# Making VectorE's lower halves of the expert weights one group later, in a one-core attention, routing and expert kernel

## The chip, the cores and the metric

The kernel runs on one core of a Trainium2 chip. A core has a matrix engine (TensorE, PE in the profile), VectorE (DVE), ScalarE (ACT), GpSimd (POOL) and a sync engine (SP) that mostly starts DMAs. Each engine works through its own instruction list in order; semaphores make one wait for another. The metric is the device time of one execution in microseconds (us), lower is better.

## What is computed

The reference, cut to the part that the change touches:

```python
# x: 2304 tokens of 512, from an attention stage; logits = x @ w_gate, 8 experts of 288 tokens each,
# tokens and experts matched greedily by descending logit
for e in range(8):
    h = np.maximum(x[mask_e] @ w1[e], 0.0)     # 512 -> 1024
    out[mask_e] = h @ w2[e]                    # 1024 -> 512
h = out @ w_in                                 # 512 -> 2048
g = np.maximum(h, 0.0) + np.log1p(np.exp(-np.abs(h)))   # softplus
return g @ w_out                               # 2048 -> 512
```

## The kernel before

Attention runs first (to about 205 us), then one pass over the experts e = 0 to 7, each with its 288 tokens. Every fp32 matrix is split in two fp32r tiles: an **upper half**, written by a ScalarE copy that rounds, and a **lower half**, which VectorE makes as the difference of the original and the upper half. A product is three matmuls into one PSUM bank (`mm3`, lines 913 to 915): upper by upper, upper by lower, lower by upper. In an expert product L913 and L914 need only the upper half of the weights, and L915 needs the lower half too.

Expert e has two loops:

- The **first loop** has 8 iterations. Iteration i makes hidden block i + 2 (`H1`: 12 matmuls into a bank of a ring of three, then a ScalarE Relu as upper half and a VectorE instruction, L1103, as lower half) and adds block i to the result (`Y`, 12 matmuls). Before `H1` it splits block i + 3 of `w1`, and after it block i + 4 of `w2` (i + 2 for expert 1).
- The **second loop** has 16 iterations. Iteration i makes block i + 2 of the second product (`H2`, 12 matmuls into the same ring), puts block i through softplus and adds it to the output (`O`). Softplus is three ScalarE functions, then `upper()`: VectorE L1148 and a ScalarE copy L1149, and `lower()`: VectorE L1157, which is also the last reader of the bank. In iterations 10 to 13 the next expert's tokens are transposed through a ring bank (`xpose`, L1075, and its VectorE half L1081), and in 9 to 15 the first blocks of the next expert's `w1` and `w2` are split. Iterations 14 and 15 hold the next expert's `H1` of blocks 0 and 1.

`split_w` (ScalarE L1026, VectorE L1029) reads a raw block that `load_w` brought from HBM. There are two raw buffers for `w1` and two for `w2`, so the load of block n + 2 can start when the lower half of block n is made. These loads are issued by SP. GpSimd issues the loads of the output weights `wo` (512 KB each), which start when `O` frees a buffer.

Between these, `tick` interleaves the **router**, which finds the next expert's tokens while this one computes. A router step of the **long kind** is a PE matmul L707 and a VectorE chain from L709 to L682; one of the **short kind** is five small PE matmuls L690 and a VectorE chain L694, L700, L702. L690 needs the result of L682, and L707 that of L702. Each half of an iteration has one `tick`, some of them empty. The router has finished for all experts at about 715 us.

`then` appends a VectorE instruction to a list when the list is in use, and `now` works the list off. Before the change it holds the lower halves of `H1` and of the transposes.

Of the kernel before, what the change touches and what calls it, by code (L numbers as in the profile page):

```python
# [8 lines left out]
F32 = mybir.dt.float32  # L9
# [5 lines left out]
ALU = mybir.AluOpType  # L15
# [544 lines left out]
class Router:  # L560


    def __init__(r, g, pool, work, bank, ring):
        r.g, r.pool, r.work, r.ring = g, pool, work, ring
        nc = g.nc
        r.n = 0
        r.idxk = g.rcf[:, 0:18]
        r.steps = [g.rcf[:, 18 + 32 * i : 50 + 32 * i] for i in range(5)]
        r.rank = g.rcf[:, 178:186]
        r.eix = g.rcf[:, 186:194]  # L570
        r.iota = g.rcf[:, 194:322]
        r.last32 = g.rcf[:, 322:323]
        r.ones16 = g.rch[:, 0:128]
        r.own4 = g.rch[:, 128:132]
        r.fine = False
        r.tri = g.rcb[:, 0:128]
        r.ones = g.rcb[:, 128:256]
        r.warm = g.rcb[:, 0:256]
        r.uw = g.rcb[:, 256:292].rearrange("p (c k) -> p c k", k=2)

        r.bank, r.used = bank, 0
        r.L = pool.tile([P, NCOL, E], F32, name="rL")
        big = r.place(31 * E + 32)
        r.oh0 = big[:, 0 : NCOL * E].rearrange("p (c e) -> p c e", e=E)
        r.m = big[:, 144:162]
        r.col = big[:, 162 : 162 + E]
        r.cnt = big[:, 0 : 31 * E]
        r.part = big[:, 31 * E :]
        r.own31 = r.place(31)
        r.key, r.loi, r.hi, r.lo, r.inc, r.free, r.pos, r.blk, r.pp = (r.place(NCOL) for _ in range(9))  # L590
        r.full, r.kp, r.pc, r.pn = r.place(E), r.place(E), r.place(E), r.place(1)
        r.pi = r.place(6)
        nc.vector.tensor_copy(r.own31, g.rch[:, 132:163])
        r.x = pool.tile([P, 5, E], F16, name="rx")
        nc.gpsimd.memset(r.x, 0.0)
        r.now = g.L
        r.k = pool.tile([P, E], F32, name="rk")
        r.kneg = pool.tile([P, 2, E], BF, name="rkneg")
        nc.gpsimd.memset(r.kneg[:, 0], -float(CAP))
        nc.gpsimd.memset(r.kneg[:, 1], 0.0)  # L600
        nc.gpsimd.memset(r.k, float(CAP))
        r.row = pool.tile([P, P], BF, name="rrow")
        nc.gpsimd.memset(r.row, 0.0)
        nc.gpsimd.memset(r.row[0:1, :], 1.0)
        r.cmp = pool.tile([P, 2, 9 * 32 + 96], BF, name="rcmp")
        nc.gpsimd.memset(r.cmp[:, :, 9 * 32 :], 0.0)
        r.all = pool.tile([P, 5 * P], BF, name="rall")
        nc.gpsimd.memset(r.all[:, NCOL * 32 :], 0.0)
        r.pw = pool.tile([P, 5, P], BF, name="rpw")
        nc.gpsimd.memset(r.pw, 0.0)  # L610
        for i in range(5):
            nc.gpsimd.memset(r.pw[0:31, i, :], float(32**i))
        r.asg = pool.tile([P, NCOL, E], BF, name="rasg")
        nc.gpsimd.memset(r.asg, 0.0)
# [259 lines left out]
class FFN:  # L874
# [141 lines left out]
            )  # L1016
        (f.w1 if which == 1 else f.w2)[e, fb] = raw

    def split_w(f, e, which, fb):
        nc = f.nc  # L1020
        d = f.w1 if which == 1 else f.w2
        raw = d[e, fb]

        tag = "w1" if which == 1 else "wo" if e and (8 * e + fb) % 5 < 3 else "w2"
        h = f.t([P, 2, 512], F32R, tag, 2 if tag == "w2" else 3)
        nc.scalar.activation(h[:, 0], raw, AF.Copy)  # L1026

        if e:
            nc.vector.tensor_tensor(h[:, 1], raw, h[:, 0].bitcast(F32), op=ALU.subtract)  # L1029
        else:  # L1030
            for c in (slice(0, 256), slice(256, 512)):
                nc.gpsimd.tensor_tensor(h[:, 1, c], raw[:, c], h[:, 0, c].bitcast(F32), op=ALU.subtract)
        d[e, fb] = h[:, 0], h[:, 1]

    def split_out(f, e, fb):

# [181 lines left out]
    def run(f):  # L1218
        nc = f.nc
# [37 lines left out]
        def tails(i):  # L1257

            if i == TL - 2:
                for _ in range(3):  # L1260
                    f.load_tail()
            if i >= TL:
                if f.ntail == 4 * NG - 4:
                    need(24)
                    f.wl = f.last()
                if f.ntail < 4 * NG:
                    f.late += 0.6 if f.ntail >= TP else 0.0
                    f.split_tail()
# [36 lines left out]
        f.tails, f.ntail = [], 0  # L1305
        for e in range(STOP):
            more = e + 1 < E
            if e:
                f.late_ops = []
            for i in range(8):  # L1310
                if i + 3 < 8:
                    f.split_w(e, 1, i + 3)
                if i + 5 < 8:
                    f.load_w(e, 1, i + 5)
                if i + 2 < 8:
                    f.H1(e, i + 2)
                tick(0.4, i < 7, e > 1)
                f.now()
                a = 4 if e > 1 else 2
                if e and i + a < 8:  # L1320
                    f.split_w(e, 2, i + a)
                if e == 0:
                    tails(i - 8)
                f.Y(e, i)
                if i % 2:
                    f.load_out(16 * e + 4 + i // 2)
                if not e and i + a < 8:
                    f.split_w(e, 2, i + a)
                if i + a + 2 < 8:
                    f.load_w(e, 2, i + a + 2)  # L1330
                if i < 7:
                    tick(0.0, True, e > 1)
            f.evac_y()
# [12 lines left out]
            for i in range(16):  # L1346
# [4 lines left out]
                elif more:  # L1351
                    f.H1(e + 1, i - 14)
                tick(0.0, i < 15, False, e == 0)
                f.now()
                if e == 0 and i + 2 < 16:
                    f.split_out(e, i + 2)
                    f.G()
                if e and i + 1 < 16:
                    f.lower()
                if e == 0:  # L1360
                    tails(i)
                    need(2 * i + 9 + LD)
# [12 lines left out]
                if more:  # L1375
                    if i == (U1 if e else U0):
                        until(e + 1)
                        f.gather(e + 1)
                        f.first_w(e + 1)
                    a, b = (10, 11) if e else (11, 14)  # L1380
                    if e and i >= 9:
                        w = (1, 0), (2, 0), (1, 1), (2, 1), (1, 2), (2, 2), (2, 3)
                        f.split_w(e + 1, *w[i - 9])
                        f.load_w(e + 1, w[i - 9][0], w[i - 9][1] + 2)
                    if not e and a <= i < a + 3:
                        f.split_w(e + 1, 1, i - a)
                        f.load_w(e + 1, 1, i - a + 2)
                    if not e and b <= i:
                        f.split_w(e + 1, 2, i - b)
                        f.load_w(e + 1, 2, i - b + 2)  # L1390
                if e == 0 and 8 <= i < 12:
                    f.load_out(i + 8)
            f.evac_o(e)
# [50 lines left out]
```

## Time and profile before

| | |
|---|---|
| median of 3 runs | 918.45 us (915.64 to 919.82) |
| profiled execution | 918.4 us, of which 916.4 us are its span |
| mean granted TensorE clock | 0.963 of 2.4 GHz |
| PE busy | 837.3 us, 91% of the span, 7152 matmuls |
| DVE busy | 595.3 us, 65% |
| ACT busy | 470.6 us, 51% |
| POOL busy | 292.4 us, 32% |

The profiled execution lies 0.05 us from the median and is taken as its picture. First loops begin about where ScalarE and VectorE copy out the output of the expert before (for experts 1 to 7 at 313.1, 403.0, 488.1, 581.1, 666.4, 751.6 and 827.4 us) and end with the split of their result (at 340.3, 426.6, 511.4, 605.2, 694.4, 773.0 and 849.1 us); the second loops lie between. A matmul's row ends by a model, later than the next one's usual start, so lateness on PE is read from start to start: 0.13 us from one matmul of 288 columns to the next, 0.23 us of 512.

### The profile page before, as it was taken

The page shows a single profiled execution, that of the slowest core. Times are in us where ns is not written, and L with a number is a line of the kernel's source. Part 1 is how long each engine was busy: PE and PEld are TensorE (multiplying, and loading weights), DVE is VectorE, ACT ScalarE, POOL GpSimd, SP SyncE. Part 2 cuts the span into 40 slices and gives each one's busy share as a digit, 9 for nine tenths or more (in the row PEclk, how much of TensorE's full clock was granted, in tenths as well). Part 3 has the DMA queues.
Part 4 walks back from the last instruction along what each step waited for, and adds up shares of the span by engine and source line. Part 5 has one row for each costly group of instructions (what it writes and reads, how often), then busy time and mean ns, then how long its engine had stood idle before and what let it go on. Part 6 is the DMA issues. An engine that isn't in the chain of part 4 may idle for free.

```text
span 916.4 us, 19578 instructions
## 1 busy us (share of the span) xinstructions
PE 837.3 (91%) x7152; PEld 740.0 (81%) x7152; DVE 595.3 (65%) x1700; ACT 470.6 (51%) x1187; POOL 292.4 (32%) x483
## 2 busy tenths in 40 slices
PE   8796989748898999989999999999889999999996
PEld 6675778637886888879878987898789899989985
DVE  4586968698867787666767565767766763344322
ACT  4675767315575535544554444445534564663542
POOL 7567431218866303310321131114101420321211
PEclk9998989859999999999999999999999999999998
DMA  9988888835256926750766165618552864665330
GB/s 256 263 264 271 247 241 269 275 113 147 93 207 244 288 70 183 208 184 27 226 179 197 46 203 157 196 28 263 149 174 56 248 202 142 184 187 185 98 109 35
DMA packets 91039, 163.03 MB, mean 178 GB/s; under 512 B 9448, under 2 KB 46824, under 8 KB 90560
## 3 DMA queue, kind: packets, MB, share of 16 engines
q1 hardware_dynamic: 66688, 85.71, 30.0%
q0 software_dynamic: 19104, 68.17, 25.0%
q10 hardware_dynamic: 5152, 7.92, 3.1%
q8 instruction: 56, 0.92, 0.4%
q14 instruction: 39, 0.32, 0.1%
HBM read 140.66 MB, written 21.10 MB: 177 GB/s over the span
## 4 chain that ended last, share of the span: by engine, by line
PE 63%; DMA 13%; DVE 13%; issue 5%; ACT 4%; POOL 2%; SPq 0%; ACTq 0%; DVEq 0%; POOLq 0%
PE ring L913 9%; PE ring L915 9%; PE acc L913 9%; PE ring L914 9%; PE acc L914 8%; PE acc L915 8%; DMA raw<-in_w_dram 5%; DMA vraw<-in_vr_dram 2%; DMA craw<-in_wout_dram 2%; PE SD L314 1%; DVE w L1029 1%; PE OD L341 1%; DMA xr<-xs,ridx 1%; PE TD L332 1%; ACT w L1026 1%
## 5 line engine op out<-in xcount | busy, mean ns | idle before, releaser
L1159 POOL CAST rem<-hh 128x64 fp32r<-128x64 f32 x128 | 32.5, 254 | 419.0 <-DVE hh L1157 407.7
L1149 ACT ACTIVATE hh<-ring 128x288 fp32r<-128x288 f32 x128 | 52.7, 412 | 134.3 <-DVE ring L1148 125.7
L913 PE MATMUL ring<-yth,wih 128*128 128x288 f32 x384 | 115.5, 301 | 0.0
L914 PE MATMUL ring<-ytl,wih 128*128 128x288 f32 x384 | 113.7, 296 | 0.8 <-DVE ytl L1123 0.8
L915 PE MATMUL ring<-yth,wil 128*128 128x288 f32 x384 | 112.9, 294 | 0.0
L913 PE MATMUL acc<-wo,hh 128*128 128x512 f32 x256 | 106.3, 415 | 0.0
L1148 DVE SCALAR_TENSOR_TENSOR ring<-ring,t 128x288 f32<-128x288 f32 x128 | 59.0, 461 | 72.7 <-ACT t L1137 72.0
L915 PE MATMUL acc<-wo,hh 128*128 128x512 f32 x256 | 100.8, 394 | 0.7 <-DVE hh L1157 0.7
L914 PE MATMUL acc<-wo,hh 128*128 128x512 f32 x256 | 100.6, 393 | 0.0
L913 PE MATMUL ring<-xgh,w 128*128 128x288 f32 x256 | 78.5, 307 | 4.1 <-DVE hh L1157 2.3
L915 PE MATMUL ring<-xgh,w 128*128 128x288 f32 x256 | 76.9, 300 | 4.0 <-DVE w L1029 3.1
L1157 DVE TENSOR_TENSOR hh<-ring,hh 128x288 fp32r<-128x288 f32 x128 | 58.0, 454 | 31.3 <-ACT hh L1149 30.4
L1051 POOL DMA_DIRECT2D wo<-wh x112 | 60.6, 543 | 55.6 <-PE acc L915 37.1
L1135 ACT ACTIVATE t<-ring 128x288 f32<-128x288 f32 x128 | 52.3, 409 | 49.2 <-PE ring L915 47.6
L1029 DVE TENSOR_TENSOR w<-raw,w 128x512 fp32r<-128x512 f32 x79 | 54.1, 689 | 35.6 <-ACT w L1026 35.1
L914 PE MATMUL ring<-xgl,w 128*128 128x288 f32 x256 | 76.1, 297 | 1.2 <-DVE xgl L1081 1.2
L913 PEld LDWEIGHTS ring<-yth,wih 128*128 128x128 f32 x384 | 72.2, 188 | 3.2 <-issue 1.3
L914 PEld LDWEIGHTS ring<-ytl,wih 128*128 128x128 f32 x384 | 72.2, 188 | 3.0 <-DVE ytl L1123 1.3
L1026 ACT ACTIVATE w<-raw 128x512 fp32r<-128x512 f32 x95 | 58.6, 626 | 29.6 <-DMA raw<-in_w_dram 25.6
L915 PEld LDWEIGHTS ring<-yth,wil 128*128 128x128 f32 x384 | 72.4, 188 | 0.0
L1101 ACT ACTIVATE hh<-ring 128x288 fp32r<-128x288 f32 x64 | 26.2, 409 | 80.6 <-PE ring L915 80.1
L1136 ACT ACTIVATE t<-t 128x288 f32<-128x288 f32 x128 | 57.0, 445 | 4.0
(245 smaller groups left out, 2295.6 us busy)
## 6 DMA issues: line engine op xcount, KB each, us to landing
wo<-wh POOLq DMA_DIRECT2D x112, 512.0 KB, 4.2
raw<-in_w_dram SPq DMA_DIRECT2D x128, 256.0 KB
craw<-in_wout_dram SPq DMA_DIRECT2D x16, 512.0 KB
wh<-wo SPq DMA_DIRECT2D x16, 512.0 KB
vz<-in_vw_dram ACTq DMA_DIRECT2D x36, 142.2 KB
vraw<-in_vr_dram SPq DMA_DIRECT2D x16, 288.0 KB
dnx<-dn SPq DMA_DIRECT2D x36, 128.0 KB
qg<-in_qc_dram SPq DMA_DIRECT2D x11, 384.0 KB
```

The costliest lines, as they stand in the source:

```text
L913: nc.tensor.matmul(o, a[0], b[0], start=start, stop=False)
L914: nc.tensor.matmul(o, a[0], b[1], start=False, stop=False)
L915: nc.tensor.matmul(o, a[1], b[0], start=False, stop=stop)
L1026: nc.scalar.activation(h[:, 0], raw, AF.Copy)
L1029: nc.vector.tensor_tensor(h[:, 1], raw, h[:, 0].bitcast(F32), op=ALU.subtract)
L1051: f.nc.gpsimd.dma_start(out=h, in_=f.g.wh[:, fb])
L1135: nc.scalar.activation(t1, o, AF.Abs)
L1136: nc.scalar.activation(t2, t1, AF.Exp, scale=-1.0)
L1148: nc.vector.scalar_tensor_tensor(o, o, 0.0, t1, op0=ALU.max, op1=ALU.add)
L1149: nc.scalar.activation(h[:, 0], o, AF.Copy)
L1157: nc.vector.tensor_tensor(h[:, 1], o, h[:, 0].bitcast(F32), op=ALU.subtract)
L1159: nc.gpsimd.tensor_copy(f.rem[fb][:, :, c : c + 32], h[:, :, 2 * P : CAP])
```

## The change

- `split_w` still issues ScalarE's upper half at once, but the VectorE lower half, with the load that follows it, goes into the list of `then` (for expert 0 there is no list and nothing changes). The list runs at the next `now`: half an iteration to an iteration later, behind the router step of the `tick` that stands ahead of that `now`.
- In the second loop `lower()` is called ahead of `now` and no longer behind it.
- The list is made once, ahead of expert 1, and not anew for each expert, so that an entry of the last iteration is carried over.
- One copy of 31 columns at the router's start (`r.own31`) moves from VectorE to ScalarE.

```diff
-        nc.vector.tensor_copy(r.own31, g.rch[:, 132:163])
+        nc.scalar.copy(r.own31, g.rch[:, 132:163])
...
-    def split_w(f, e, which, fb):
+    def split_w(f, e, which, fb, load=8):
...
         nc.scalar.activation(h[:, 0], raw, AF.Copy)
 
-        if e:
-            nc.vector.tensor_tensor(h[:, 1], raw, h[:, 0].bitcast(F32), op=ALU.subtract)
-        else:
...
-        d[e, fb] = h[:, 0], h[:, 1]
+        def rest():
+            if e:
+                nc.vector.tensor_tensor(h[:, 1], raw, h[:, 0].bitcast(F32), op=ALU.subtract)
+            else:
...
+            d[e, fb] = h[:, 0], h[:, 1]
+            if load < 8:
+                f.load_w(e, which, load)
+
+        f.then(rest)
...
-            if e:
+            if e == 1:
                 f.late_ops = []
             for i in range(8):
                 if i + 3 < 8:
-                    f.split_w(e, 1, i + 3)
-                if i + 5 < 8:
-                    f.load_w(e, 1, i + 5)
+                    f.split_w(e, 1, i + 3, i + 5)
...
                 tick(0.0, i < 15, False, e == 0)
+                if e and i + 1 < 16:
+                    f.lower()
                 f.now()
                 if e == 0 and i + 2 < 16:
                     f.split_out(e, i + 2)
                     f.G()
-                if e and i + 1 < 16:
-                    f.lower()
```

On PE, SP and GpSimd the sequence of instructions is the same in both kernels, the DMAs that they issue among them; on ScalarE the one copy is added. Only VectorE's sequence differs. Three places follow; with the change L1029 is counted as L1030, and the lines from `xhalves` to softplus 5 higher (L1157 is L1162).

VectorE in the second loop of expert 1, iterations 11 and 12, before: `w1_314` is a weight block, `ring_309` and `hh_313` are softplus, `rt_1` to `rall` a long router step.

```order
L1148 SCALAR_TENSOR_TENSOR ring_309_5875<-ring_309_5875,t1_310_5888 128x288
L1029 TENSOR_TENSOR w1_314_5922<-raw1_290_5728,w1_314_5922 128x512
L709 TENSOR_REDUCE rt_1_2932<-rt_1_2932 128x31
L712 TENSOR_SCALAR rjunk154_5947,rhit155_5948<-rt_1_2932 128x31
L675 SCALAR_TENSOR_TENSOR rt_1_2932<-rhit155_5948,rt_1_2932 128x18
L682 TENSOR_TENSOR rall_2947<-rt_1_2932,rcf_79 128x576
L1157 TENSOR_TENSOR hh_313_5919<-ring_309_5875,hh_313_5919 128x288
L1081 TENSOR_TENSOR xgl_2959<-ring_319_5954,xgh_2958 128x288
```

The same place with the change:

```order
L1153 SCALAR_TENSOR_TENSOR ring_308_5872<-ring_308_5872,t1_309_5885 128x288
L709 TENSOR_REDUCE rt_1_2932<-rt_1_2932 128x31
L712 TENSOR_SCALAR rjunk154_5944,rhit155_5945<-rt_1_2932 128x31
L675 SCALAR_TENSOR_TENSOR rt_1_2932<-rhit155_5945,rt_1_2932 128x18
L682 TENSOR_TENSOR rall_2947<-rt_1_2932,rcf_79 128x576
L1162 TENSOR_TENSOR hh_313_5919<-ring_308_5872,hh_313_5919 128x288
L1030 TENSOR_TENSOR w1_314_5922<-raw1_290_5728,w1_314_5922 128x512
L1086 TENSOR_TENSOR xgl_2959<-ring_319_5954,xgh_2958 128x288
```

The lower half of `w1_314` stood ahead of the router step and of softplus's lower half, and now stands behind both.

VectorE in the first loop of expert 4, iterations 2 and 3, before: `w1_605` is block 6, which the `H1` of iteration 4 multiplies, and `hh_607` the lower half of the `H1` of iteration 3.

```order
L1103 SCALAR_TENSOR_TENSOR hh_603_8482<-ring_602_8469,hh_603_8482 128x288
L1029 TENSOR_TENSOR w2_604_8495<-raw2_593_8415,w2_604_8495 128x512
L1029 TENSOR_TENSOR w1_605_8510<-raw1_595_8427,w1_605_8510 128x512
L709 TENSOR_REDUCE rt_1_2932<-rt_1_2932 128x31
L712 TENSOR_SCALAR rjunk283_8530,rhit284_8531<-rt_1_2932 128x31
L675 SCALAR_TENSOR_TENSOR rt_1_2932<-rhit284_8531,rt_1_2932 128x18
L682 TENSOR_TENSOR rall_2947<-rt_1_2932,rcf_79 128x576
L1103 SCALAR_TENSOR_TENSOR hh_607_8526<-ring_606_8513,hh_607_8526 128x288
```

With the change:

```order
L1108 SCALAR_TENSOR_TENSOR hh_601_8476<-ring_600_8463,hh_601_8476 128x288
L709 TENSOR_REDUCE rt_1_2932<-rt_1_2932 128x31
L712 TENSOR_SCALAR rjunk283_8528,rhit284_8529<-rt_1_2932 128x31
L675 SCALAR_TENSOR_TENSOR rt_1_2932<-rhit284_8529,rt_1_2932 128x18
L682 TENSOR_TENSOR rall_2947<-rt_1_2932,rcf_79 128x576
L1030 TENSOR_TENSOR w2_604_8495<-raw2_596_8439,w2_604_8495 128x512
L1030 TENSOR_TENSOR w1_605_8509<-raw1_597_8442,w1_605_8509 128x512
L1108 SCALAR_TENSOR_TENSOR hh_607_8524<-ring_606_8511,hh_607_8524 128x288
```

Both weight halves moved behind the long router step of iteration 3.

VectorE in the first loop of expert 5, iterations 0 and 1, before: `w2_714` is block 4 of `w2`, and `w1_717` block 4 of `w1`, which the `H1` of iteration 2 multiplies.

```order
L1103 SCALAR_TENSOR_TENSOR hh_713_9495<-ring_712_9482,hh_713_9495 128x288
L1029 TENSOR_TENSOR w2_714_9508<-raw2_703_9443,w2_714_9508 128x512
L709 TENSOR_REDUCE rt_1_2932<-rt_1_2932 128x31
L712 TENSOR_SCALAR rjunk337_9531,rhit338_9532<-rt_1_2932 128x31
L675 SCALAR_TENSOR_TENSOR rt_1_2932<-rhit338_9532,rt_1_2932 128x18
L682 TENSOR_TENSOR rall_2947<-rt_1_2932,rcf_79 128x576
L1029 TENSOR_TENSOR w1_717_9536<-raw1_699_9394,w1_717_9536 128x512
L1103 SCALAR_TENSOR_TENSOR hh_720_9554<-ring_719_9541,hh_720_9554 128x288
```

With the change:

```order
L1108 SCALAR_TENSOR_TENSOR hh_711_9489<-ring_710_9476,hh_711_9489 128x288
L709 TENSOR_REDUCE rt_1_2932<-rt_1_2932 128x31
L712 TENSOR_SCALAR rjunk337_9528,rhit338_9529<-rt_1_2932 128x31
L675 SCALAR_TENSOR_TENSOR rt_1_2932<-rhit338_9529,rt_1_2932 128x18
L682 TENSOR_TENSOR rall_2947<-rt_1_2932,rcf_79 128x576
L1030 TENSOR_TENSOR w2_714_9508<-raw2_705_9458,w2_714_9508 128x512
L1030 TENSOR_TENSOR w1_716_9533<-raw1_701_9421,w1_716_9533 128x512
L1108 SCALAR_TENSOR_TENSOR hh_718_9548<-ring_717_9535,hh_718_9548 128x288
```

The router step moved ahead of `w2_714`, whose raw block comes by DMA.

## Rows read from the trace of the kernel before

**Rows 1.** Windows: length, busy PE, PEld, DVE, ACT, POOL, clock, DMA share, GB/s.

```profile
313.00:720.00 407.00, 387.64 (x2681) 345.56 (x2680) 282.87 (x866) 189.35 (x442) 78.50 (x175) 0.99 0.52 157
720.00:908.00 188.00, 187.81 (x1196) 172.60 (x1195) 79.12 (x179) 98.33 (x226) 38.85 (x90) 1.00 0.51 150
```

**Rows 2.** Waits of PE, 313 to 720 us: sum, times, longest; idle over 0.15.

```profile
PE ring L913 <- DVE hh L1157: 4.6, 5, 1.3
PE rt L707 <- DVE ry L702: 3.0, 2, 2.6
...
PE acc L915 <- DVE hh L1157: 0.7, 1, 0.7
```

**Rows 3.** Timeline, second loop of expert 1, iterations 11 and 12: start, duration, instruction, idle before.

```profile
386.93 0.46 DVE L1148 SCALAR_TENSOR_TENSOR ring<-ring,t 128x288 f32<-128x288 f32 x1
...
387.52 0.28 PE L707 MATMUL rt<-ry,rch 128*128 128x248 f16 x1
...
388.44 0.69 DVE L1029 TENSOR_TENSOR w<-raw,w 128x512 fp32r<-128x512 f32 x1 [1.05 <-ACT w L1026]
...
389.05 0.42 DVE L709 TENSOR_REDUCE rt<-rt 128x31 f32<-128x248 f32 x1
...
389.38 0.40 PE L915 MATMUL acc<-wo,hh 128*128 128x512 f32 x1
...
390.63 0.45 DVE L1157 TENSOR_TENSOR hh<-ring,hh 128x288 fp32r<-128x288 f32 x1
...
391.13 0.41 PE L913 MATMUL ring<-yth,wlh 128*128 128x288 f32 x1 [1.35 <-DVE hh L1157]
```

**Rows 4.** Timelines of ACT, DVE and PE, first loop of expert 5, iterations 0 to 2.

```profile
673.51 1.15 ACT L1026 ACTIVATE w<-raw 128x512 fp32r<-128x512 f32 x2 [5.02 <-DMA raw<-in_w_dram]
...
668.51 0.17 DVE L694 TENSOR_TENSOR rx<-rt,rch 128x32 f16<-128x32 f32 x1
...
669.31 0.45 DVE L1103 SCALAR_TENSOR_TENSOR hh<-ring,hh 128x288 fp32r<-128x288 f32 x1
674.17 0.69 DVE L1029 TENSOR_TENSOR w<-raw,w 128x512 fp32r<-128x512 f32 x1 [4.41 <-ACT w L1026]
674.78 0.42 DVE L709 TENSOR_REDUCE rt<-rt 128x31 f32<-128x248 f32 x1
...
676.35 0.68 DVE L1029 TENSOR_TENSOR w<-raw,w 128x512 fp32r<-128x512 f32 x1
...
677.09 0.40 PE L915 MATMUL ring<-xgh,w 128*128 128x288 f32 x1 [1.84 <-DVE w L1029]
```

**Rows 5.** Timeline, first loop of expert 1, iterations 1 and 2.

```profile
320.23 0.69 DVE L1029 TENSOR_TENSOR wo<-raw,wo 128x512 fp32r<-128x512 f32 x1 [2.96 <-DMA raw<-in_w_dram]
...
322.76 0.29 PE L915 MATMUL ring<-xgh,w 128*128 128x288 f32 x1
```

**Rows 6.** Windows after those two places, and one at the start of expert 3.

```profile
324.00:327.00 3.00, 3.00 (x14) 3.00 (x14) 2.40 (x5) 1.45 (x3) 0.00 (x0) 0.50 0.35 108
679.00:682.00 3.00, 3.00 (x14) 3.00 (x14) 2.29 (x6) 1.30 (x3) 0.00 (x0) 0.50 0.68 202
...
488.00:494.00 6.00, 6.00 (x51) 5.85 (x50) 5.77 (x16) 3.09 (x6) 1.55 (x3) 1.00 0.98 314
```

**Rows 7.** Timeline, first loop of expert 4, iterations 3 and 4.

```profile
594.31 0.28 PE L707 MATMUL rt<-ry,rch 128*128 128x248 f16 x1
...
594.63 0.42 DVE L709 TENSOR_REDUCE rt<-rt 128x31 f32<-128x248 f32 x1 [0.92 <-PE rt L707]
...
596.22 0.45 DVE L1103 SCALAR_TENSOR_TENSOR hh<-ring,hh 128x288 fp32r<-128x288 f32 x1
596.32 0.30 PE L915 MATMUL ring<-xgh,w 128*128 128x288 f32 x1
```

**Rows 8.** Timelines of SP and ACT, first loop of expert 3.

```profile
489.95 0.38 SPq L1009 DMA_DIRECT2D raw<-in_w_dram  x1
...
497.67 0.63 ACT L1026 ACTIVATE w<-raw 128x512 fp32r<-128x512 f32 x1 [2.24 <-DMA raw<-in_w_dram]
```

More of the change, by code (lines that the diff above doesn't have):

```diff
@@ L1026, in split_w @@
         nc.scalar.activation(h[:, 0], raw, AF.Copy)
-        if e:
-            nc.vector.tensor_tensor(h[:, 1], raw, h[:, 0].bitcast(F32), op=ALU.subtract)
-        else:
-            for c in (slice(0, 256), slice(256, 512)):
-                nc.gpsimd.tensor_tensor(h[:, 1, c], raw[:, c], h[:, 0, c].bitcast(F32), op=ALU.subtract)
-        d[e, fb] = h[:, 0], h[:, 1]
+        def rest():
+            if e:
+                nc.vector.tensor_tensor(h[:, 1], raw, h[:, 0].bitcast(F32), op=ALU.subtract)
+            else:
+                for c in (slice(0, 256), slice(256, 512)):
+                    nc.gpsimd.tensor_tensor(h[:, 1, c], raw[:, c], h[:, 0, c].bitcast(F32), op=ALU.subtract)
+            d[e, fb] = h[:, 0], h[:, 1]
+            if load < 8:
+                f.load_w(e, which, load)
+        f.then(rest)
     def split_out(f, e, fb):
@@ L1320, in run @@
                 if e and i + a < 8:
-                    f.split_w(e, 2, i + a)
+                    f.split_w(e, 2, i + a, i + a + 2)
                 if e == 0:
@@ L1327, in run @@
                 if not e and i + a < 8:
-                    f.split_w(e, 2, i + a)
-                if i + a + 2 < 8:
-                    f.load_w(e, 2, i + a + 2)
+                    f.split_w(e, 2, i + a, i + a + 2)
                 if i < 7:
@@ L1382, in run @@
                         w = (1, 0), (2, 0), (1, 1), (2, 1), (1, 2), (2, 2), (2, 3)
-                        f.split_w(e + 1, *w[i - 9])
-                        f.load_w(e + 1, w[i - 9][0], w[i - 9][1] + 2)
+                        f.split_w(e + 1, *w[i - 9], w[i - 9][1] + 2)
                     if not e and a <= i < a + 3:
-                        f.split_w(e + 1, 1, i - a)
-                        f.load_w(e + 1, 1, i - a + 2)
+                        f.split_w(e + 1, 1, i - a, i - a + 2)
                     if not e and b <= i:
-                        f.split_w(e + 1, 2, i - b)
-                        f.load_w(e + 1, 2, i - b + 2)
+                        f.split_w(e + 1, 2, i - b, i - b + 2)
                 if e == 0 and 8 <= i < 12:
```

## The prediction

> **What bounds the kernel now.** I read the windows first, to see where there is anything to win. From 720 us to 908 us TensorE is busy for 187.81 of 188 us, while from 313 to 720 us, where the router works beside experts 1 to 5, it is busy for 387.64 of 407 [rows 1]. So the matrix engine sets the time, some 19 us of it are idle in the second stretch, and only there can a new order on VectorE change anything. Expert 0 has no list, and the order of experts 6 and 7 has no router steps to get past.
>
> The waits of PE come next. Two kinds bear on the change [rows 2]: six waits of 5.3 us together for L1157, softplus's lower half, which frees a bank of the ring or feeds `O`; and 3.0 us of L707 for the router's L702, of which one is 2.6. For the working I then went to the timelines, engine by engine, at one place of each kind.
>
> **What softplus's lower half gains.** In the second loop VectorE does L1148 (ends at 387.39), then has nothing until ScalarE has made the weights' upper half: idle 1.05, lower half from 388.44, and only then the router step at 389.05, L1157 at 390.63, and PE's first matmul into the freed bank at 391.13 [rows 3]. PE was ready at 389.38 + 0.23 = 389.61, so it was 1.52 late. With the change the router step follows L1148 directly. Its input is L707, begun at 387.52; the step can start 0.32 behind that (594.31 to 594.63 in [rows 7]), at 387.84 and not 389.05: 1.21 earlier. L1157 and the bank move with it, and 0.31 of the lateness stays, because the router step itself is still ahead. The weights' lower half takes its 0.6 behind L1157, where the idle 1.05 was, so the rest of the iteration is not later.
>
> The six waits read 5.3, and the timed one reads 1.35 for 1.52 late, 0.17 less; 5.3 + 6 x 0.17 = 6.3. At 1.21 of 1.52 that gives 5.0. Waits under 0.15 are not in that view and a few short ones of the same kind must exist, so I take **5.5**. The bounds: 3.2 (half of 6.3, if the router's PE matmul leaves more than here) and 6.3. Transposes that wait for L1081 behind a router step keep their place, and I count nothing for them.
>
> **What the first loops gain.** Two of them have one DMA wait that blocks everything behind it. For expert 5 ScalarE waits 5.02 for a raw block, and VectorE 4.41 behind it, at the lower half of a `w2` block that is needed only two iterations later. The router step behind it starts at 674.78 and the lower half of `w1`, for which PE waits 1.84, at 676.35 [rows 4]. With the change the router step has run before, in the idle 4.41, and the two lower halves follow ScalarE's: 674.17 + 0.60 + 0.69 = 675.46, and L915 0.06 behind it, at 675.5 and not 677.09: 1.58 gained. In the next iteration a short router step now stands ahead of the weights and costs about 0.4 (below): **1.2**. For expert 1 the block lands at 320.23, and L915 comes at 322.76, behind a router step and the 2.6 of L707 [rows 2, 5]. By the same sum it comes at 320.23 + 0.60 + 0.69 + 0.06 = 321.58, 1.18 earlier. Expert 1 splits `w2` later than the others, so that two of its last `Y` now wait behind router steps, about 0.6 (an estimate, one lower half of 0.6): **0.6**.
>
> After both idle stretches the granted clock falls to 0.50, the lower level of 1.2 GHz: 14 matmuls in 3 us, against 51 in 6 us at 1.00 [rows 6]. That is (25.5 - 14)/25.5 x 3 = 1.35 us lost each. The stall of 1.35 in [rows 3] was followed by no such stretch. With the change the waits of 1.84 and 2.6 that stood ahead of them shrink to 0.3 and about 1.4, the latter in two places, so I expect both slow stretches to vanish: **2.7**, or 0 if what is left of idle is still enough.
>
> **What it costs.** In the first loop `w1` block i + 3 is multiplied one iteration later, right behind `Y`. Its lower half was made ahead of the router step, and now comes behind it and behind a `w2` block. In expert 4, iteration 3, L707 begins at 594.31, the long step runs from 594.63 to 596.22, then 0.60 and 0.69: ready at 597.51. Before, the first L915 of the next `H1` came at 596.32 with no wait [rows 7]. It is **1.24** late. The router's period puts a long step at this iteration in experts 3, 4 and 5: 3.7. A short step takes 0.32 + 0.80 (668.51 to 669.31 in [rows 4]) + 0.60 + 0.69 = 2.41, against the 2.01 from 594.31 to 596.32: 0.4 late, which I count for expert 2 (0.5 with a remainder at its start) and have counted for expert 5. Elsewhere in experts 2 to 4 these delays at iterations 0 to 2 lie under waits for raw blocks that end at the same time as before (next part), so they cost nothing; if that cover goes, they are 1.2 for expert 2 and 0.8 each for 3 and 4. The bounds of this part are 0 (if ScalarE and PE run so late that the lower halves are ready anyway) and 4.2 + 2.8 = 7.0.
>
> **The loads.** Each deferred lower half takes the load of the block two further on with it. SP's order stays, and nothing else stands behind them on SP at that place, but at a first loop's start two loads are issued some 2 to 3 us later (a router step of 0.8 or 1.6 and two lower halves). For expert 3, a `w1` load issued at 489.95 is awaited by ScalarE until 497.67, 7.7 us, and in the first 6 of them the DMA engines are busy for 0.98 of the time at 314 GB/s, with GpSimd's output weights [rows 6, 8]. A block issued in the middle of that burst lands at its end; issued 2 us later, but still inside, it should land at the same end, and I take **0**, with 1.9 for each of experts 2, 3 and 4 as the other bound. The Trainium skill speaks against my value: "DMA: Bandwidth & Descriptors", Queues, rings and completion order, says that each DMA engine takes turns between the queues that have work, packet by packet. By that a load on SP's queue does not stand behind GpSimd's queue, so that one issued later lands later by as much, and the sum would lose the 5.7 of the first rival below. The 7.7 us in a burst of 314 GB/s speak for the burst's end.
>
> The copy of 31 columns lies before expert 0, one small instruction moved between two engines: at most 0.2 either way, taken as 0.
>
> **Sum.** 5.5 + 1.2 + 0.6 + 2.7 - 3.7 - 0.5 = 5.8 gained. The profiled execution took 918.4 (the median is 918.45), so **912.6 us**.
>
> **The rivals.** *The loads land later* (same): experts 2, 3 and 4 wait 1.9 longer each, 5.7 in all, and the time is 918.3. For it: these first loops are bound by landings. Against it: the saturated DMA above. *The new waits start slow stretches* (slower): the place is iterations 1 to 3 of the first loops of experts 2 to 5, where late loads and lower halves behind router steps add up. If a block lands 3 us later than before, PE idles as long as at 319 and 673 us, and each place costs 3.0 + 1.35; at four places, 17.4, and without the 2.7 won back: 912.6 + 17.4 + 2.7 = 932.7. With two such places it is about 924. It decides if one of the new waits grows as long as the 2.6 of [rows 2], behind which such a stretch stood. Against it: at each place the landing that now ends last is one that has been issued while DMA was full. *The costs stay hidden* (faster still): experts 3 to 5 wait for raw blocks long enough that the 3.7 vanish: 908.9, and at the bounds of the other parts 906.5. *The change does nothing*: waits of 5.3 sit elsewhere by the time they are removed, as PE then waits for the router: 918.4. Against it: the timed place, where the router's input is early by 1.21.
>
> **Chances and range.** My forecast 0.55, the costs hidden 0.10, the loads late 0.22, nothing 0.06, slower 0.07. The forecast's own bounds run from 906.5 (6.3 + 2.8 + 2.7 with no cost) to 916; with the two cases near 918.4 the range is 906.5 to 919. A difference of 0.5%, 4.6 us, is about what a measurement of this kernel can tell. Faster by more (under 913.8): most of the forecast and all of the hidden case, 0.58. Within 0.5%: 0.35. Slower: 0.07.
>
> **What the profile of the changed kernel would show.** Waits for softplus's lower half (now L1162) fall from 5.3 to under 2. VectorE's weight halves no longer wait for ScalarE in the second loop. No stretch of clock 0.50 between 313 and 720 us. New waits of PE's L915 for the weights' lower half, 1.0 to 1.3 each, in iteration 4 of experts 3, 4 and 5. ScalarE's waits for raw blocks end, relative to the loop's start, where they did. The prediction is wrong if those landings move by over a microsecond, if a slow stretch of the clock remains, or if the router's L690 and L707 wait in place of L913.

## The result, and the profile after

The changed kernel takes 912.0 us (median of 18 runs, 908.95 to 919.16) against 921.0 for the kernel before (18 runs beside it, 915.64 to 929.65): ratio 0.9907, 95% interval 0.9883 to 0.9931, or 8.6 us less (6.4 to 10.8). The prediction was 912.6, from a sum of 5.8. The profiled execution took 914.7 us, 3.7 less than that of before; from expert 1's first `Y` matmul to the end of the last matmul it is 6.0 shorter (594.3 to 588.3), while the part ahead of it, in which the copy of 31 columns is all that differs, took 2.6 longer.

The windows of the changed kernel (columns as in [rows 1]):

```profile
313.00:720.00 407.00, 392.50 (x2718) 348.54 (x2718) 289.43 (x887) 192.57 (x449) 88.06 (x177) 1.00 0.53 160
...
295.00:298.00 3.00, 3.00 (x9) 2.43 (x10) 0.82 (x2) 0.38 (x2) 0.82 (x3) 0.50 1.05 384
...
321.00:324.00 3.00, 2.90 (x26) 2.51 (x24) 2.08 (x6) 1.98 (x5) 0.00 (x0) 1.00 0.50 167
...
674.00:677.00 3.00, 2.76 (x25) 2.45 (x24) 2.40 (x6) 1.60 (x3) 0.00 (x0) 1.00 0.34 105
```

PE is idle for 14.5 us of the 407 instead of 19.4, and the two stretches of [rows 6] are gone: its clock is 1.00 behind both places (321 and 674 us) and over the window. One stretch at 0.50 stands at 295, in expert 0. The waits of PE in the same window (sum, times, longest), first a line of before that [rows 2] leaves out, then two of the changed kernel:

```profile
PE ring L915 <- DVE w L1029: 2.9, 4, 1.8
```

```profile
PE ring L915 <- DVE w L1030: 6.4, 10, 1.1
...
PE ring L913 <- ACT w L1026: 1.2, 2, 0.6
```

Both kinds of [rows 2] are off the list; in their place the waits for the weights' lower half have grown from four of 2.9 us together to ten of 6.4. The timeline at the place of [rows 3]:

```profile
387.08 0.46 DVE L1153 SCALAR_TENSOR_TENSOR ring<-ring,t 128x288 f32<-128x288 f32 x1
387.70 0.42 DVE L709 TENSOR_REDUCE rt<-rt 128x31 f32<-128x248 f32 x1 [0.17 <-PE rt L707]
...
389.28 0.45 DVE L1162 TENSOR_TENSOR hh<-ring,hh 128x288 fp32r<-128x288 f32 x1
389.65 0.68 DVE L1030 TENSOR_TENSOR w<-raw,w 128x512 fp32r<-128x512 f32 x1
...
389.79 0.41 PE L913 MATMUL ring<-yth,wlh 128*128 128x288 f32 x1
```

The router step starts 0.62 behind the start of L1153 and not 2.12; L1162 comes right behind it, and the weights' half after that. PE's L915 before began at 389.25, so that its L913 is 0.31 late instead of 1.52, as the working had it.

First loop of expert 5, the place of [rows 4]:

```profile
670.66 1.15 ACT L1026 ACTIVATE w<-raw 128x512 fp32r<-128x512 f32 x2 [4.45 <-DMA raw<-in_w_dram]
...
668.25 0.41 DVE L709 TENSOR_REDUCE rt<-rt 128x31 f32<-128x248 f32 x1
...
671.32 1.29 DVE L1030 TENSOR_TENSOR w<-raw,w 128x512 fp32r<-128x512 f32 x2 [1.42 <-ACT w L1026]
...
672.67 0.40 PE L915 MATMUL ring<-xgh,w 128*128 128x288 f32 x1 [0.28 <-DVE w L1030]
```

The long router step now runs while ScalarE waits for its block, and VectorE's idle time is 1.42, not 4.41. L915 comes 7.00 us behind the loop's first `Y` matmul (at 665.67) and not 9.13.

In expert 1, where L707 waited 2.59 [rows 5], 0.90 is left:

```profile
320.08 0.41 PE L915 MATMUL ring<-xgh,w 128*128 128x288 f32 x1 [0.90 <-DVE w L1030]
...
322.69 0.69 DVE L1030 TENSOR_TENSOR wo<-raw,wo 128x512 fp32r<-128x512 f32 x1
```

The `w2` half now stands behind the router step and waits for no DMA. The price shows in expert 4 [rows 7]:

```profile
593.14 0.42 DVE L709 TENSOR_REDUCE rt<-rt 128x31 f32<-128x248 f32 x1 [1.45 <-PE rt L707]
...
594.72 1.28 DVE L1030 TENSOR_TENSOR w<-raw,w 128x512 fp32r<-128x512 f32 x2
...
596.06 0.41 PE L915 MATMUL ring<-xgh,w 128*128 128x288 f32 x1 [1.08 <-DVE w L1030]
```

Two lower halves run behind the long step, and L915 is 1.08 late against the row, 1.24 from start to start.

Expert 3's first loop went another way than forecast. The timelines of SP, GpSimd and ScalarE at its start, before and then after (its first `Y` matmul is at 489.61 and 486.77):

```profile
487.42 1.31 SPq L1014 DMA_DIRECT2D raw<-in_w_dram  x2
487.43 2.12 POOL L1051 DMA_DIRECT2D wo<-wh  x4
490.23 1.15 ACT L1026 ACTIVATE w<-raw 128x512 fp32r<-128x512 f32 x2
...
494.79 0.63 ACT L1026 ACTIVATE w<-raw 128x512 fp32r<-128x512 f32 x1 [1.11 <-DMA raw<-in_w_dram]
```

```profile
483.95 0.37 SPq L1009 DMA_DIRECT2D raw<-in_w_dram  x1
483.96 2.11 POOL L1056 DMA_DIRECT2D wo<-wh  x4
484.92 3.92 SPq L1014 DMA_DIRECT2D raw<-in_w_dram  x2
491.71 1.15 ACT L1026 ACTIVATE w<-raw 128x512 fp32r<-128x512 f32 x2 [4.41 <-DMA raw<-in_w_dram]
```

Before, the raw block 4 of `w2` (L1014) went out 0.01 us ahead of GpSimd's four output weights, and ScalarE used it 2.8 us later. After, it goes out 0.96 behind the first of the four, and ScalarE has waited 4.41 when it comes, 6.8 us after the issue. The kernel before has such a case too: its second L1014 load, block 5, went out 0.96 behind the first of the four and was used at 494.79, 6.4 us later.

### The profile page after: what moved, and what is told of

Same layout as the page of the kernel before. It is cut to its first block, busy times and chain, and to the rows that moved or that the text cites. A ratio compares the mean times of both kernels' runs of the same rounds, so it can differ in the third digit from the quotient of the medians.

```text
span 913.0 us, 19550 instructions
## 1 busy us (share of the span) xinstructions
PE 837.0 (92%) x7152; PEld 737.7 (81%) x7152; DVE 595.2 (65%) x1699; ACT 471.1 (52%) x1188; POOL 305.4 (33%) x483
## 3 DMA queue, kind: packets, MB, share of 16 engines
q1 hardware_dynamic: 66688, 85.71, 30.4%
q0 software_dynamic: 19104, 68.17, 24.8%
## 4 chain that ended last, share of the span: by engine, by line
PE 58%; DVE 15%; DMA 13%; issue 5%; POOL 4%; ACT 4%; SPq 0%; ACTq 0%; DVEq 0%; POOLq 0%
PE ring L915 9%; PE ring L913 9%; PE ring L914 9%; PE acc L913 9%; PE acc L914 8%; PE acc L915 8%; DMA raw<-in_w_dram 3%; DMA craw<-in_wout_dram 2%; DMA vraw<-in_vr_dram 2%; DMA xr<-xs,ridx 2%; DVE w L1030 2%; DMA vz<-in_vw_dram 1%; DMA dnx<-dn 1%; DVE rt L709 1%; PE ring L1080 1%
## 5 line engine op out<-in xcount | busy, mean ns | idle before, releaser
L1164 POOL CAST rem<-hh 128x64 fp32r<-128x64 f32 x128 | 46.1, 360 | 394.0 <-DVE hh L1162 391.3
L913 PE MATMUL ring<-yth,wih 128*128 128x288 f32 x384 | 115.5, 301 | 0.0
L915 PE MATMUL ring<-yth,wil 128*128 128x288 f32 x384 | 112.9, 294 | 0.0
L913 PE MATMUL acc<-wo,hh 128*128 128x512 f32 x256 | 106.7, 417 | 0.0
L1153 DVE SCALAR_TENSOR_TENSOR ring<-ring,t 128x288 f32<-128x288 f32 x128 | 59.0, 461 | 72.7 <-ACT t L1142 72.1
L915 PE MATMUL acc<-wo,hh 128*128 128x512 f32 x256 | 101.2, 395 | 0.0
L915 PE MATMUL ring<-xgh,w 128*128 128x288 f32 x256 | 77.7, 303 | 8.2 <-DVE w L1030 6.7
L1162 DVE TENSOR_TENSOR hh<-ring,hh 128x288 fp32r<-128x288 f32 x128 | 58.2, 455 | 41.0 <-ACT hh L1154 40.0
L913 PE MATMUL ring<-xgh,w 128*128 128x288 f32 x256 | 78.2, 305 | 1.4 <-ACT w L1026 1.2
L913 PEld LDWEIGHTS ring<-yth,wih 128*128 128x128 f32 x384 | 72.2, 188 | 3.2 <-issue 1.3
L915 PEld LDWEIGHTS ring<-yth,wil 128*128 128x128 f32 x384 | 72.4, 189 | 0.0
L1141 ACT ACTIVATE t<-t 128x288 f32<-128x288 f32 x128 | 56.9, 445 | 4.0
L1142 ACT ACTIVATE t<-t 128x288 f32<-128x288 f32 x128 | 56.9, 445 | 4.1
```

The source lines that it names most:

```text
L913: nc.tensor.matmul(o, a[0], b[0], start=start, stop=False)
L915: nc.tensor.matmul(o, a[1], b[0], start=False, stop=stop)
L1141: nc.scalar.activation(t2, t1, AF.Exp, scale=-1.0)
L1142: nc.scalar.activation(t1, t2, AF.Ln, bias=1.0)
L1153: nc.vector.scalar_tensor_tensor(o, o, 0.0, t1, op0=ALU.max, op1=ALU.add)
L1162: nc.vector.tensor_tensor(h[:, 1], o, h[:, 0].bitcast(F32), op=ALU.subtract)
```

## The experiments

The table puts the profiled executions side by side. A first loop is counted from its first `Y` to the first `H2` matmul, a second loop from there to the next `Y`; the second loops of experts 1 to 4 are summed.

| kernel | ratio to before, 95% | second loops | first loops of experts 1, 2, 3, 4, 5 | their sum |
|---|---|---|---|---|
| before | 1 | 257.6 | 26.8, 23.2, 22.9, 22.9, 27.5 | 123.3 |
| the change | 0.9907 (0.9883 to 0.9931) | 250.8 | 24.5, 23.6, 25.6, 24.2, 25.6 | 123.5 |
| copy alone | 1.0005 (0.9980 to 1.0030) | 257.7 | 26.4, 23.3, 22.8, 23.0, 27.8 | 123.3 |
| second loop alone | 0.9974 (0.9945 to 1.0004) | 251.6 | 25.3, 23.2, 26.9, 25.9, 27.0 | 128.1 |
| first loop alone | 1.0001 (0.9970 to 1.0032) | 257.6 | 24.8, 23.2, 24.0, 23.8, 26.5 | 122.3 |
| list first | 0.9967 (0.9928 to 1.0007) | 254.8 | 24.4, 23.6, 24.2, 24.2, 26.5 | 122.9 |
| w1 at once | 0.9884 (0.9849 to 0.9920) | 250.8 | 26.9, 23.1, 24.0, 23.2, 23.7 | 120.9 |
| second loop alone, end at once | 0.9976 (0.9943 to 1.0010) | 250.8 | 27.1, 22.9, 27.0, 23.7, 28.0 | 128.8 |
| w1 at once, end at once | 0.9831 (0.9782 to 0.9880) | 250.8 | 26.6, 22.9, 23.7, 21.9, 23.8 | 118.8 |
| the same, expert 1 deferred | 0.9821 (0.9772 to 0.9870) | 250.8 | 24.4, 23.2, 23.6, 22.2, 24.0 | 117.4 |
| the same, output weights by SP | 0.9774 (0.9737 to 0.9810) | 250.8 | 24.4, 21.9, 22.0, 21.9, 22.0 | 112.2 |
| second loop alone, output weights moved | 1.0281 (1.0244 to 1.0319) | 250.8 | 25.1, 30.1, 28.5, 27.8, 29.3 | 140.8 |
| the change, output weights moved | 1.0320 (1.0271 to 1.0370) | 250.8 | 24.4, 29.9, 31.0, 28.7, 30.4 | 144.5 |
| w1 at once, end at once, expert 1 deferred, output weights moved | 1.0222 (1.0172 to 1.0271) | 250.9 | 24.4, 28.9, 28.8, 26.4, 30.9 | 139.5 |

**The copy alone.**

```diff
-        nc.vector.tensor_copy(r.own31, g.rch[:, 132:163])
+        nc.scalar.copy(r.own31, g.rch[:, 132:163])
```

> The kernel before with nothing but the copy of 31 columns moved from VectorE to ScalarE. The prediction counts 0 for it: within 0.5 us of before, ratio 0.9995 to 1.0005. The rival is that a small shift at the router's start moves the later chance of half-clock stretches, which would show as 2 us or more either way.

Measured: 921.23 us, 1.0005. The copy is worth nothing that can be measured.

**Each loop's part alone.** `split_w` gets a switch; with `False` the lower half and the load follow at once.

```diff
# second loop alone
-                    f.split_w(e, 1, i + 3, i + 5)
+                    f.split_w(e, 1, i + 3, i + 5, False)
# and the same for both calls of split_w for w2 in the first loop
```

> The lower halves of the weights are deferred in the second loop alone (softplus's lower half ahead of the list there); in the first loop they are made at once, as before. Theory A (the second loop holds the gain, since there a bank no longer waits for a weight half and a router step; the first loop's gains and losses cancel): the traces of the two kernels differ by 6.8 us in the second loops of experts 1 to 4, so the time is 6 to 7 us below before, ratio 0.993. Theory B (the gain is the first loop's, by the router step getting past a lower half that waits for a DMA, and by the half-clock stretches that stood behind such waits): the time stays within 2 us of before, ratio 0.998 or more, and the profile shows the 5 us wait of expert 5 and half-clock stretches again.

```diff
# first loop alone; lower() behind now() again
-                        f.split_w(e + 1, *w[i - 9], w[i - 9][1] + 2)
+                        f.split_w(e + 1, *w[i - 9], w[i - 9][1] + 2, False)
```

> The other part alone: deferred in the first loop, the second loop as before. Theory A: gains of 1.2 and 0.6 and two half-clock stretches (2.7) against 1.24 late three or four times and a load behind the output weights in expert 3: within 2 us of before, ratio 0.998 to 1.002, with waits of 1.24 of L915 for the weights' lower half in its profile and 1.3 to 1.4 of L913 for softplus's lower half back in the second loop. Theory B: 5 us or more below before, ratio 0.994 or less.

Measured: 920.38 us and 921.06 us. The second was as theory A had it. The first was not: the interval takes in no change, so that by ratio theory B looks right. The stages say something else. The second loops did gain 6.0 us, and the first loops gave 4.8 of it back: those of experts 3 and 4 grew by 4.0 and 2.9. The waits (310 to 720 us), the timelines of ScalarE, VectorE and PE in expert 3, and two windows show how:

```profile
PE ring L915 <- DVE w L1030: 5.8, 4, 1.9
PE rt L707 <- DVE ry L702: 2.6, 1, 2.6
```

```profile
494.03 1.15 ACT L1026 ACTIVATE w<-raw 128x512 fp32r<-128x512 f32 x2 [4.47 <-DMA raw<-in_w_dram]
...
494.69 0.69 DVE L1030 TENSOR_TENSOR w<-raw,w 128x512 fp32r<-128x512 f32 x1 [3.57 <-ACT w L1026]
495.30 0.42 DVE L709 TENSOR_REDUCE rt<-rt 128x31 f32<-128x248 f32 x1
...
497.62 0.41 PE L915 MATMUL ring<-xgh,w 128*128 128x288 f32 x1 [1.85 <-DVE w L1030]
```

```profile
499.00:501.00 2.00, 2.00 (x13) 1.85 (x13) 1.21 (x5) 1.29 (x3) 0.00 (x0) 0.50 0.75 218
595.00:597.00 2.00, 2.00 (x11) 2.00 (x10) 1.85 (x6) 1.37 (x3) 0.00 (x0) 0.50 0.97 236
```

The raw block comes late, as in the changed kernel. But here VectorE waits 3.57 for it ahead of the router step, the `w1` half behind that is 1.85 late for PE, and a stretch of clock 0.50 follows, in experts 3 and 4 (and in 5, at 680). So the deferral of the second loop makes these first loops worse, and that of the first loop takes it back: by itself it saves 1.0 in the first loops, beside the other 4.7 (128.1 to 123.5). The parts do not add up because each changes what the other is worth.

**The list ahead of softplus's lower half.**

```diff
-                if e and i + 1 < 16:
-                    f.lower()
                 f.now()
...
+                if e and i + 1 < 16:
+                    f.lower()
```

> As the changed kernel, but softplus's lower half stays behind the list, as before the change. By the prediction's sum what frees the bank is that the weights' half is no longer ahead of the router step (1.21), and lower() ahead of the list saves the one weight half of 0.6 more; so at the five or six places where 0.31 of lateness is left it would be 0.9, the second loops of experts 1 to 4 are 3.0 to 3.6 us longer than with the change and the ratio to before is 0.994 to 0.995. The rival is that the order of the two does not matter, because the bank is freed in time either way: 0.991.

Measured: 920.07 us, 0.9967 with an interval that holds the expected range. The second loops are 4.0 longer than with the change (3.0 to 3.6 were expected), and the wait is back (PE, 310 to 720 us):

```profile
PE ring L913 <- DVE hh L1162: 2.8, 4, 0.7
```

So of the 6.8 that the second loops gain, 4.0 need `lower()` ahead of the list; 2.9 come from the weights' half behind the router step alone.

This kernel also shows what happened in expert 3. SP, GpSimd and ScalarE at the start of its first loop (first `Y` at 487.43):

```profile
485.22 4.27 SPq L1014 DMA_DIRECT2D raw<-in_w_dram  x2
...
485.24 2.12 POOL L1056 DMA_DIRECT2D wo<-wh  x4
...
489.09 1.15 ACT L1026 ACTIVATE w<-raw 128x512 fp32r<-128x512 f32 x2 [1.13 <-DMA raw<-in_w_dram]
```

Block 4 of `w2` goes out just ahead of GpSimd's four loads again, as before the change, and is used 3.9 us later and not 6.8. Expert 3's first loop takes 24.2 instead of 25.6, and the 1.4 come back at the `H1` behind that block; expert 4's is 24.2 in both kernels.

**`w1` at once in the first loop.**

```diff
-                    f.split_w(e, 1, i + 3, i + 5)
+                    f.split_w(e, 1, i + 3, i + 5, False)
```

> As the changed kernel, but the first loop makes w1's lower half at once; w2's, which is needed two iterations later, stays deferred, and so does all of the second loop. If the late L915 are what the first loop pays, as the prediction has it (1.24 in experts 2, 3 and 4, about 1 in expert 1, 0.4 and less at other places), they vanish and the time is 3 to 5 us below the changed kernel, ratio to before 0.986 to 0.988. If instead raw blocks' landings bound these first loops, so that the lower half's place does not matter, it is that of the changed kernel, 0.991, and PE's waits move to ScalarE's upper halves.

Measured: 910.34 us, 0.9884, just above the range for the late L915 (the intervals of this kernel and of the changed one overlap, so the times do not decide). From expert 1 to the end its trace is 3.2 us shorter than the changed kernel's. PE's waits, 310 to 720 us:

```profile
PE ring L913 <- ACT w L1026: 3.2, 4, 1.1
...
PE rt L707 <- DVE ry L702: 2.4, 1, 2.4
...
PE ring L915 <- DVE w L1030: 0.8, 4, 0.2
```

L915's waits fall from 6.4 to 0.8. In expert 1 the wait of L707 is back, with a half-clock stretch behind it, and what is left in the others is ScalarE's wait for raw blocks: both theories hold a part.

**Late loads.** Two edits in three kernels. The first edit makes the splits of iterations 14 and 15 at once, so that their loads go out as early as before; it was tried on the kernel with the second loop alone and on the one with `w1` at once. The third kernel adds to the latter that expert 1 stays deferred.

```diff
-                        f.split_w(e + 1, *w[i - 9], w[i - 9][1] + 2)
+                        f.split_w(e + 1, *w[i - 9], w[i - 9][1] + 2, i < 14)
...
-                    f.split_w(e, 1, i + 3, i + 5, False)
+                    f.split_w(e, 1, i + 3, i + 5, e == 1)
```

> The kernel deferred in the second loop alone, but the splits of iterations 14 and 15 (blocks 2 and 3 of the next expert's w2) are made at once again; no softplus half stands behind them. In the profile of the kernel without this edit the second loops of experts 1 to 4 gained 6.1 us, and the first loops of experts 3 and 4 lost 4.0 and 3.0: the load of w2's block 5 went out 3.2 us later against the loop's start, the ones beside it up to 1.5, and each loop shows a wait of 2.0 of L915 behind a router step that stands behind a late raw block. Theory A (loads issued later land later, and an instruction that waits for one blocks VectorE): with the loads back in their place the first loops of experts 3 and 4 are within 1 us of before (22.9 each), and the time is about 5 us below before, ratio 0.993 to 0.995. Theory B (the first loops lose because the second loop is shorter and the output weights' burst comes ahead of the raw blocks, whatever the load's place): they stay at 25 to 27, ratio 0.997.

> The kernel with w1 at once in the first loop, with the same edit: the splits of iterations 14 and 15 at once. Theory A: the raw waits that are left in the first loops of experts 3 and 4 (24.0 and 23.2 us long, with four waits of ScalarE's upper half of 3.2 together) shrink by 1 to 2 us together, ratio 0.986 to 0.988. Theory B, by which the place of these loads does not matter: 0.988 as without it, within 0.5 us.

> The same again, but in expert 1's first loop w1's lower half is deferred as in the changed kernel (there the loop took 24.46 us, and with w1 at once 26.93, with the wait of 2.4 of L707 and a half-clock stretch). If that wait comes from the head of the line on VectorE, expert 1's first loop is 24.5 again and the time 2.4 us below the kernel without this edit, ratio 0.983 to 0.986. The rival is that half-clock stretches come by chance and only move to another place: no difference.

Measured: 918.26 us, 907.64 and 907.56. The first is no clear gain (0.9976 with and 0.9974 without the edit): what expert 4 got back (2.1, and its half-clock stretch is gone) went again in expert 1 (1.8, where such a stretch now stands behind a wait of L707 of 3.1) and expert 5 (1.0). Expert 4's first loop falls as theory A had it (25.9 to 23.7, and 23.2 to 21.9), expert 3's stays (27.0, and 23.7 for 24.0) as theory B had it. There the raw block still goes out behind GpSimd's four loads, by 0.95 us, and ScalarE waits 4.6 and 4.4. The third kernel's expert 1 takes 24.4 instead of 26.6, with no wait of L707 and no half-clock stretch in that loop. The two medians are the same, so by time the rival, no difference, stands; the trace of the third is 1.9 shorter from expert 1 on, but ahead of that stand two half-clock stretches in expert 0, where the other has none.

**The output weights' loads.**

```diff
-                if i % 2:
+                if e > 1 and i > 3:
+                    f.load_out(16 * e + 2 * i - 8)
+                    f.load_out(16 * e + 2 * i - 7)
+                elif e < 2 and i % 2:
                     f.load_out(16 * e + 4 + i // 2)
...
-                if e and i < 12:
+                if e and i < 8:
```

> The kernel deferred in the second loop alone, and GpSimd's loads of the output weights 0 to 3 of the next expert moved from the end of the second loop to iterations 4 and 5 of the first loop, and 4 to 7 to iterations 6 and 7 (experts 2 to 7). In expert 3 the raw block of w2's block 4 was issued 0.01 us ahead of the first of four such loads before and landed in 2.8 us; with the deferral it goes out 0.95 us behind it and lands in 6.8. Theory A (the first loops of experts 3 to 5 lose because raw blocks stand behind this burst): the loops fall from 26.9, 25.9 and 27.0 us to 23 or less, the waits of 1.9 of L915 and the half-clock stretches behind them vanish, and the time is 8 us or more below before, ratio 0.991 or less. Theory B (they lose because the loads themselves are issued later, burst or not): the waits stay within 1 us, ratio 0.996 to 0.998.

> The changed kernel with the same move of the output weights' loads. Theory A: the first loop of expert 3 falls from 25.6 to about 23.9 (the 1.24 of the long router step stays, since it does not come from a load), those of 4 and 5 by up to 1 each; 3 us below the changed kernel, ratio to before 0.986 to 0.989. Theory B: no difference to the changed kernel, 0.991. If the output weights then come too late for the second loop, its O would wait for them and the time would rise by up to 5 us.

> The fastest kernel so far (w1 at once in the first loops of experts 2 to 5, splits of iterations 14 and 15 at once) with the same move. Theory A: of the 2.9 us in which PE's L913 waits for ScalarE's upper halves, nearly all goes, 3 us below that kernel, ratio to before 0.978 to 0.981. Theory B: no difference, 0.982.

Measured: 945.63 us (1.0281, 1.0244 to 1.0319), 950.63 (1.0320, 1.0271 to 1.0370) and 941.81 (1.0222, 1.0172 to 1.0271). All the expectations missed, because the edit did not do what it was to do. On GpSimd nothing in a first loop makes it wait, so it issues these loads as soon as it is through with the second loop. Expert 3 of the kernel with the second loop alone:

```profile
491.86 4.34 POOL L1059 DMA_DIRECT2D wo<-wh  x8
...
496.41 5.09 SPq L1014 DMA_DIRECT2D raw<-in_w_dram  x2
...
507.84 1.15 ACT L1026 ACTIVATE w<-raw 128x512 fp32r<-128x512 f32 x2 [6.62 <-DMA raw<-in_w_dram]
```

Eight loads in a row, where four had been, and `w2`'s block 5, issued at 496.41, is used at 507.84, 11.4 us later; with four loads (the second loop alone) it was used 6.4 after its issue. Block 4, 0.95 behind the first load in both, took 7.0 and 6.9. So the burst was made longer, and the blocks behind it later. The first loops of experts 6 and 7, which have no router, went from 21.2 and 21.9 us to 28.4 and 27.7: raw blocks behind the output weights are enough to lengthen a first loop, without any router step on VectorE.

**Output weights by SP.** In the fastest kernel so far:

```diff
-            f.nc.gpsimd.dma_start(out=h, in_=f.g.wh[:, fb])
+            if sync:
+                f.nc.sync.dma_start(out=h.bitcast(F32), in_=f.g.wh[:, fb])
+            else:
+                f.nc.gpsimd.dma_start(out=h, in_=f.g.wh[:, fb])
...
-                    f.load_out(16 * e + 4 + i // 2)
+                    f.load_out(16 * e + 4 + i // 2, True)
```

> The move in the three runs before did not delay the output weights' loads: GpSimd has nothing else to wait for in the first loop, so that eight of them went out in one piece where four had. Here the loads of output weights 4 to 7 (those issued in the first loop) stay at their place in the program but are issued by SP, on its own queue, where the raw blocks' loads ahead of them pace them; the rest is as in the kernel with w1 at once, the splits of iterations 14 and 15 at once and expert 1 deferred. Theory A (raw blocks are held up by loads issued ahead of them): w2's block 4 of expert 3, issued 1.9 us ahead of the loop's start, is there 3 us later and not 6.9, ScalarE's wait of 4.4 is under 1, the first loops of experts 2 to 5 (23.2, 23.6, 22.2, 24.0) fall by 2 to 4 together, ratio to before 0.978 to 0.980. Theory B (the total of bytes in this stretch sets the landing, in whatever order): the waits move to later raw blocks of the same loops and the time stays, 0.982, or rises.

Measured: 901.49 us, 0.9774, a little better than theory A had it. Expert 3 (first `Y` at 490.92):

```profile
489.07 1.30 SPq L1014 DMA_DIRECT2D raw<-in_w_dram  x2
...
492.03 1.15 ACT L1026 ACTIVATE w<-raw 128x512 fp32r<-128x512 f32 x2 [0.58 <-DMA raw<-in_w_dram]
...
496.28 0.37 SPq L1060 DMA_DIRECT2D wo<-wh  x1
```

The same block, issued 1.85 ahead of the loop as in the other kernels, is used 3.0 us later and not 6.8. The first loops of experts 2 to 5 fall from 23.2, 23.6, 22.2 and 24.0 to 22 each, and among PE's waits from 310 to 720 us none for ScalarE's upper halves is left (2.9 in the kernel without this edit). This version beats both kernels. The edit changes two things at once, the queue of these loads and their time (in expert 3 the first goes out 5.4 us into the loop and not 2.8 ahead of it); no run tells the two apart.

## Why the prediction came true

**The second loop.** Predicted 5.5, measured 6.8 (257.6 to 250.8). The mechanism is shown at the timed place to a hundredth (1.21 of 1.52), and the list-first run shows that softplus's order is needed for 4.0 of it. At the six waits of [rows 2] in these loops, read from start to start, 5.4 came back where the working had 5.0, since 0.31 is left at three of them only. The larger part of the difference is in the short waits that the view does not list: 0.5 was taken for them, and they gave 1.5.

**The first loops.** Predicted -0.3 (expert by expert -1.95, +0.5, +1.24, +1.24, -1.31), measured +0.2 (-2.35, +0.4, +2.7, +1.2, -1.8). Expert 4 is the step as predicted, 1.24 (the working's own numbers, 597.51 and 596.32, give 1.19, or 1.25 with the 0.06 that its other sums add). Expert 2's +0.4 is luck: its first `H1` has an L915 that is 1.24 late, which was held to be covered, and about as much came back at its other waits. Expert 5's L915 came 2.1 us earlier in its loop and not 1.58, since ScalarE's block was there 0.56 earlier. The two half-clock stretches vanished. Stretches at this place of expert 1 stand behind waits of L707 of 2.1 to 3.1 us in five of the seven traces that have such a wait there; the kernel with the second loop alone (2.6) and the same with the output weights moved (2.4) have the wait without the stretch, so 2.7 is no certain gain.

**The step that failed** is "The loads", in expert 3: 0 was taken, and 1.5 us were lost over the 1.24. In expert 4 it held: `w2`'s block 5 was issued 3.2 us later against the loop and was used 0.5 earlier. In expert 3 the load was not pushed about inside a full burst. It had been ahead of the burst by 0.01 us and came behind it, because the 0.7 of softplus's wait [rows 2], which stood 2.8 us ahead of this loop, was gone and GpSimd's loads went out 0.63 us earlier against the loop, while block 4 went out 0.34 later. With 0.97 us lost in the order, the block was in use 4.3 us later against the loop's start, which is over the microsecond that the prediction had named as a sign of being wrong. The list-first kernel, where the block is ahead again, takes 1.4 of the 1.5 back, and in the last experiment, with no burst at that place, the block issued at the same time is used 3.0 us later. That is the rival of the late loads, in one expert of three and by another way than its 1.9. The row that the working leaned on says less than it was taken for: the window of 0.98 and 314 GB/s runs from 488 to 494 us and so covers the first 4 of the 7.7 us, not 6.

The Trainium skill's rule, "DMA: Bandwidth & Descriptors", Queues, rings and completion order, is that each DMA engine takes turns between the queues with work, by packets. The rows neither bear it out nor refute it: behind eight loads instead of four ScalarE's wait for block 5 grew from 1.7 to 6.6 us, but in these kernels a `w1` load also stands on SP's queue just ahead of the `w2` block (0.97 us ahead of block 4 in the changed kernel, 3.3 before). That load alone is not the cause, since it stands there in the last experiment too. They show only that a place ahead of the burst, or no burst, is worth 3 to 4 us here.

**What was not foreseen** is the interaction: the second loop's part alone gives 2.4 us by ratio (its interval takes in 0) and the first loop's part alone nothing, but both 8.6; by the stages in the table 1.2, 1.1 and 6.6. Priced one at a time against the kernel before, as the prediction does, the first loop's deferral is worth about nothing; its worth is that it keeps a late block from holding up the router once the second loop is shorter. The prediction has no such term. Its sum came out with both parts in place, where the loss in the first loops stayed small, and by errors that cancel: expert 3 lost 1.5 more than forecast, the second loops gave 1.3 more and experts 1 and 5 together 0.9 more.

**The total.** The sum of 5.8 lies close to the 6.0 that the two traces differ by, and just below the interval of the ratio (6.4 to 10.8). By stages the traces differ by 6.6 (6.8 less 0.2), of which 0.5 went again in expert 5's second loop. The 2.6 between 6.0 and 8.6 stays open. The median of before was also 2.6 above the execution that the sum starts from; that 912.6 lies so near to 912.0 is in this part luck.

## What to carry to other kernels

On an engine that works through its list in order, put what nobody needs soon behind what another engine waits for, but split by need: the half that was needed two iterations later gained by the delay, and the one needed in the next cost up to 1.24 at a time. Before moving an instruction that a load hangs on, look at which other queue's loads go out at the same moment. Where two parts of an edit meet in one wait, try them together as well as apart.

## What the runs showed of the hardware

- A 256 KB block that is issued 0.01 us ahead of four loads of 512 KB from another engine's queue was in use 2.8 us later (3.9 in the list-first kernel); issued 0.96 behind the first of them, 6.8 us; with those loads elsewhere, 3.0 us. The next such block was in use 6.4 us after its issue behind four of those loads, and 11.4 behind eight.
- GpSimd, with nothing to wait for, issued its DMAs far ahead of their place in the program: loads written for iterations 4 to 7 went out before the loop's iteration 0 was done, at 491.86 to 496.2 with the first `Y` at 494.67.
- The kernel with the second loop alone had stretches of clock 0.50 behind two waits of PE of 1.0 and 1.9 in expert 3 and behind one of 1.9 in expert 4; single waits of 1.1 in the changed kernel had none.
